# Sliding-window attention and a gated feed-forward block on one core: the order of the prologue's small jobs, of its weight loads, and of batch 1's transposes

## The chip, the cores and the metric

The kernel runs on one core of one Trainium2 chip. The metric is the device time of one execution in microseconds (us). Three runs of the kernel before gave 339.52, 340.06 and 340.07; the median is 340.06.

The core's engines have separate instruction queues and meet through semaphores: PE (TensorE, matmuls and transposes), ACT (ScalarE, exp, Ln, gelu, copies), DVE (VectorE, products and copies), POOL (GpSimd; here above all it issues the loads that convert float32 to bf16) and SP (SyncE; it issues plain DMAs). Each queue is worked off in order, so an instruction that waits also holds up everything queued behind it on its engine.

## The reference

```
scores = q @ k.T / 8 + bias          # per batch and head; S = 576, D = 64, 8 heads, 8 batches
bias   = -slope[h] * (i - j)         # slope[h] = 2 ** -(h + 1)
scores = where(0 <= i - j < 128, scores, -1e9)
x      = softmax(scores) @ v         # put together to x[4608, 512]
out    = (gelu(x @ w_gate) * (x @ w_val)) @ w_out      # d_ff = 1536
```

All inputs and the output are float32; the kernel works in bf16 with float32 accumulation.

## The kernel before, in words

The feed-forward part is the bulk. The 4608 tokens go in nine groups g of 512. For each group and each of 12 tiles f of 128 hidden columns, `gate_val` (line 603) does four matmuls with `w_gate` and four with `w_val`, ACT makes the gelu (line 624), DVE multiplies (line 625) and leaves a hidden tile; `out_part` and `out_half` (lines 647 and 669) then multiply the hidden tiles with `w_out`. Attention for a batch is woven between these matmuls, always for tokens that a later group needs. All PSUM tiles come from one pool of eight banks (`bank`, line 66).

Heads go in pairs c = 0 to 3, with head 2c in partitions 0 to 63 and head 2c + 1 in 64 to 127. Scores need q and k transposed (`qT`, `kT`). The queries of batches 0 and 1 are loaded in "runs" (line 121): each partition holds r consecutive tokens, and after the transposes a copy out of PSUM (`untangle`, line 155, copy in line 158) puts the tokens in order. For batch 1 the first run (n = 0) is tokens 0 to 383 with r = 3, the second (n = 1) tokens 384 to 575 with r = 2.

**Prologue (lines 699 to 831).** Eight DMAs load the first 384 tokens of batch 0's q and k as float32, two heads each (line 713); seven go out on SP, the first of k on ACT. POOL makes `tmpl` (an iota), then copies two elements of the first q load into `mark` (line 720): this holds its queue back until that load has landed. After that POOL issues, in order, the rest of batch 0's q and k, v, and the weights by column ranges (lines 721 to 726): 0 to 128, 128 to 256, 256 to 512, and, further down (lines 833 to 838), 512 to 768, 768 to 1024, 1024 to 1280, then both runs of batch 1's q and k, then 1280 to 1536.

DVE makes small constants: `slope1`, `ones8`, the identity `ident`, `far`, and `dist` (the distances, with a huge number where the mask is, lines 733 to 740). `slopes` (line 748) is one 128x128 diagonal matrix for each head: one DVE product for heads 0 to 3 and one for heads 4 to 7. ACT makes the "decays", exp(-slope x distance) of each head (line 744), from `dist`.

For batch 0 each pair c passes through this: a cast of q and one of k to bf16 (`cast`, line 752, done in line 753), three transposes each (`first`, line 768, PE in line 771) and a copy each (line 158); `biases0` (line 327, PE in line 334) puts slope x distance into two banks with matmuls, `scores0` (line 339, PE in line 212) adds the scores on top, and two exps on ACT follow (line 225, 128x512 each). The code writes out by hand, in lines 792 to 824, which engine does which cast and copy, and in which order. After the four pairs come the sums (`products`), Ln and exp for the reciprocals (lines 571 and 572), the values, the rest of batch 0's scores (eight exps of 128x384), a load of ACT's gelu table, and the gate tiles f = 0 and 1 (for the first 384 tokens), then f = 2 to 8, then the same nine tiles for the other 128 tokens.

**Group 0's end (lines 923 to 953).** Gate tiles 9, 10 and 11 of group 0 are done whole. Behind tiles 9 and 11, `transpose` (line 162) transposes both runs of batch 1's q and k, two pairs at a time: ten transposes and two copies (384 and 192 columns) for each of q and k and each pair, q's copies on ACT, k's on DVE. Then the list in line 893 is worked off in order: scores of batch 1 (`scores`, line 231, s = 0 the first half of the keys, s = 1 the second; each with exps on ACT and a mask product on DVE, line 228), between them halves of the output rows 0 and 1 (`out_half`, six matmuls each, a copy to `osb` in line 679 behind the second half).

Of the kernel before, what the change touches and what calls it, by code (L numbers as in the profile page):

```python
# [8 lines left out]
BF16 = mybir.dt.bfloat16  # L9
AF = mybir.ActivationFunctionType  # L10
ALU = mybir.AluOpType
# [19 lines left out]
def kernel(  # L31
# [34 lines left out]
    def bank():  # L66
        return psum.tile([128, 512], FP32, name="ps")
# [62 lines left out]
    def load_runs(b, n, h0, h1):  # L130
        first, parts, r = RUNS[b][n]
        for what, src in ((0, q), (1, k)):
            nc.gpsimd.dma_start(
                out=runs(what, b, n)[:, h0:h1, :],
                in_=src[b][h0:h1, first:first + parts * r, :].rearrange(
                    "h (p r) d -> p h (r d)", r=r))

    def load_w(lo, hi):
        for dst, src in ((wg, moe_w_gate), (wv, moe_w_val)):
            nc.gpsimd.dma_start(  # L140
                out=dst[:, :, lo:hi],
                in_=src[:, lo:hi].rearrange("(c p) f -> p c f", p=128))

    def transpose_runs(b, n, what, c, ps):
        first, parts, r = RUNS[b][n]
        src = runs(what, b, n)
        p = 64 * what if (b, n) == (0, 1) else 0
        for x in range(r):
            for i in (0, 1):
                nc.tensor.transpose(  # L150
                    out=ps[64 * i:64 * i + 64, parts * x:parts * x + parts],
                    in_=src[:, 2 * c + i, 64 * x:64 * x + 64],
                    identity=ident[p:p + parts, p:p + parts])

    def untangle(copy, b, n, what, c0, c1, ps):
        first, parts, r = RUNS[b][n]
        m = c1 - c0
        copy(out=(qT, kT)[what][b][:, c0:c1, first:first + parts * r].rearrange(
                 "p c (x r) -> p c x r", r=r),
             in_=ps[:, 0:m * parts * r].rearrange("p (c r x) -> p c x r", c=m, r=r))  # L160

    def transpose(b, what, c, copy):
        ps = bank().bitcast(BF16)
        for n, lo in ((0, 0), (1, 384)):
            transpose_runs(b, n, what, c, ps[:, lo:576])
        for n, lo in ((0, 0), (1, 384)):
            untangle(copy, b, n, what, c, c + 1, ps[:, lo:576])

    def transposes_dma(b):
        def of_k():  # L170
# [539 lines left out]
    pairs1 = wo[:, 9:12, :]  # L710
    for h in (0, 2, 4, 6):
        for w, src in ((0, q), (1, k)):
            (nc.scalar if w and h == 0 else nc.sync).dma_start(  # L713
                out=raw[w][h // 4].rearrange("p (h x) -> p h x", h=4)[:, h % 4:h % 4 + 2, :],
                in_=src[0][h:h + 2, 0:384, :].rearrange("h (p r) d -> p h (r d)", r=3))

    nc.gpsimd.iota(tmpl, pattern=[[1, 256]], base=0, channel_multiplier=-1,
                   allow_small_or_imprecise_dtypes=True)
    nc.gpsimd.memset(ones64, 1.0)
    nc.gpsimd.tensor_copy(out=mark, in_=raw[0][0][0:1, 0:2])  # L720
    load_runs(0, 1, 0, 8)
    load_v(0, (0, 1, 2))
    load_w(0, 128)
    load_w(128, 256)
    load_v(0, (3, 4))
    load_w(256, 512)

    for h in range(H):
        nc.vector.memset(slope1[:, h:h + 1], -8.0 * 2.0 ** (-8.0 * (h + 1) / H))
    nc.vector.memset(ones8, 0.0)  # L730
    nc.vector.memset(ones8.rearrange("p (h x) -> p h x", x=40)[:, :, 0:8], 1.0)
    nc.vector.tensor_single_scalar(out=ident, in_=tmpl[:, 0:128], scalar=0.0, op=ALU.is_equal)
    for lo, bound, op in ((0, 0.0, ALU.is_lt), (128, 127.5, ALU.is_gt)):
        nc.vector.tensor_scalar(out=far[:, lo:lo + 128], in0=tmpl[:, lo:lo + 128],
                                scalar1=bound, scalar2=1e9, op0=op, op1=ALU.mult)
# [2 lines left out]
        nc.vector.tensor_tensor(out=dist[half, 0:192], in0=tmpl[half, to], in1=far[half, to], op=ALU.max)  # L738
    for to, n in ((192, 192), (384, 128)):
        nc.vector.tensor_copy(out=dist[:, to:to + n], in_=dist[:, 0:n])  # L740

    def decays(lo, hi):
        for h in range(lo, hi):
            nc.scalar.activation(out=emask[:, h, 0:192], in_=dist[:, 0:192], func=AF.Exp,
                                 scale=-(2.0 ** (-8.0 * (h + 1) / H)))

    def made_slopes(lo, hi):
        nc.vector.tensor_tensor(
            out=slopes[:, lo:hi, :], in0=ident.unsqueeze(1).to_broadcast((128, hi - lo, 128)),
            in1=slope1[:, lo:hi].unsqueeze(2).to_broadcast((128, hi - lo, 128)), op=ALU.mult)  # L750

    def cast(w, c, copy):
        copy(out=pairs0[w][:, :, c, :].rearrange("p x (i d) -> p x i d", i=2),
             in_=raw[w][c // 2].rearrange("p (c i x d) -> p c x i d", c=2, i=2, x=3)[:, c % 2])

    made_slopes(0, 4)

    def masks_of_last_blocks(lo, hi):
        nc.vector.tensor_copy(out=emask[:, lo:hi, 192:384], in_=emask[:, lo:hi, 0:192])
# [8 lines left out]
    def first(w, c, copy, ps):  # L768
        ps = ps.bitcast(BF16)
        for x in range(3):  # L770
            nc.tensor.transpose(out=ps[:, 128 * x:128 * x + 128], in_=pairs0[w][:, x, c, :],
                                identity=ident)
        untangle(copy, 0, 0, w, c, c + 1, ps)
# [19 lines left out]
    held = [bank(), bank()]  # L793
    keep_busy(held[0], 2, 128)
    keep_busy(held[0], 60)
    decays(0, 5)
    cast(0, 0, dve)
    cast(1, 0, act)
    made_slopes(4, 8)
    decays(5, 7)  # L800
    first(0, 0, dve, held[0])
    first(1, 0, act, held[1])
    cast(0, 1, dve)
    cast(1, 1, act)
    decays(7, 8)

    def pair(c, copies, between=None):
        held = [bank(), bank()]
        for w in (0, 1):
            first(w, c, copies[w], held[w])  # L810
            if w == 0 and between:
                between()

    cast(0, 2, dve)
    cast(1, 2, dve)
    scores0((0,), biases0((0,), 4), lambda: pair(1, (dve, act)))
    cast(1, 3, act)
    biases = biases0((1,))
    pair(2, (dve, dve), lambda: cast(0, 3, dve))
    scores0((1,), biases)  # L820
    biases = biases0((2,))
    pair(3, (dve, dve))
    scores0((2,), biases)
    scores0((3,), biases0((3,)))
    row(0)
    sums_a = products(0, sums_first(0))
# [6 lines left out]
    load_w(512, 768)  # L833
    load_w(768, 1024)
    load_w(1024, 1280)
    for n in (0, 1):
        load_runs(1, n, 0, 8)
    load_w(1280, DFF)
    masks, waiting = [], []

    def flush():
# [44 lines left out]
    for t in (qs[0], ks[0]):  # L886
# [3 lines left out]

    acts = (act, act, act, act)
    todo = {
        0: [("table",), ("s", 1, 0, (0, 1)), ("o", 0, 0, 0), ("o", 0, 1, 0), ("s", 1, 0, (2, 3)), ("o", 0, 0, 1), ("s", 1, 1, (0, 1)), ("o", 0, 1, 1), ("s", 1, 1, (2, 3), masks), ("pv+", 1, 0), 4, ("transposes", 2), ("pv+", 1, 1), 4],
        1: [("table",), ("s", 2, 0, (0, 1)), 3, ("s", 2, 0, (2, 3)), 2, ("s", 2, 1, (0, 1)), 2, ("s", 2, 1, (2, 3), masks), ("pv+", 2, 0), 3, ("pv+", 2, 1), 1, 2, ("s2", 3, 0), ("add", 3, 0), 3, ("s2", 3, 2), ("add", 3, 2, None, (0,))],
    }

# [12 lines left out]
    def exp_table():  # L909
        nc.scalar.preload_act_table_set("natural_log_exp_and_others")  # L910

    RUN = {"s": scores, "s2": scores2, "add": add, "sum4": sums4, "gather": gather, "spread": spread_dma, "pv": values, "pv+": values_and_sums,
           "masks": flush, "table": exp_table, "transposes": transposes_dma, "last": out_last, "o": out_half}

    for g in range(NG):
        if 1 <= g < B - 2:
            transposes_dma(3 if g == 1 else g + 2)
        if g == 1:

            nc.gpsimd.tensor_copy(out=mark, in_=kT[1][0:1, 0, 512:514])  # L920
            load_qk(4)
            load_v(3)
        for f in range(9 if g == 0 else 0, NF):
            gate_val(g, f)
            if g == 2 and f == 2:
                add(3, 2, act, (1,))
            if g == 0 and f == 10:
                masks_of_last_blocks(0, 8)
            if g == 0 and f in (9, 11):
                for c in (0, 1) if f == 9 else (2, 3):  # L930
                    for w in (0, 1):
                        transpose(1, w, c, (act, dve)[w])
            if 2 <= g < B - 1:
                if f == (4 if g == 2 else 3):
                    sums4(g + 1)
                if f == (6 if g == 2 else 5):
                    gather(g + 1)
                if f == (8 if g == 2 else 7):
                    spread_dma(g + 1)
                if f == 9 and g + 2 < B:  # L940

                    nc.gpsimd.tensor_copy(out=mark, in_=hid[g][0:1, f, 0:2])  # L942
                    if g + 3 < B:
                        load_qk(g + 3)
                    load_v(g + 2)
        if g == 0:
            nc.gpsimd.memset(Ps[0][:, :, 0:64], 0.0)
            for t in (qs[1], ks[1]):
                nc.gpsimd.memset(t[64:128, 4, :], 0.0)
        for item in steps(g):  # L950
            if isinstance(item, int):
                out_part(g, item)
            else:
                RUN[item[0]](*item[1:])
        store()
        if g == 0:

            nc.gpsimd.tensor_copy(out=mark, in_=qT[0][0:1, 0, 512:514])
            load_qk(3)
            load_v(2)  # L960
# [30 lines left out]
```

## Time and profile before

| what | us |
|---|---|
| median of three runs | 340.06 |
| the profiled execution's own time | 339.51 |
| its span | 337.70 |
| PE busy | 331.6 |
| DVE busy | 192.3 |
| ACT busy | 172.0 |
| POOL busy | 106.6 |
| first Ln of the prologue (line 571) starts | 12.31 |
| gate tile f = 2 starts | 21.02 |
| first scores of batch 1 start | 41.80 |
| group 1 starts | 58.12 |

The span runs from the first to the last instruction of the profiled execution; its own time has 1.81 us more around it. A row of a timeline gives start, duration, engine, line, operation and the tiles that are written and read; "x6" merges six in a row, and a bracket tells how long the engine had been idle and for whom. Instructions on one engine overlap a little: the next can start about 0.1 us before the former's end. The time of a DMA to its landing is counted from the issue on its queue to its completion.

### The profile page before, as it was taken

The numbers are of one execution on the slowest core, as the hardware profiler recorded it, in microseconds if no ns is written. First come the engines' busy times: TensorE is split into PE (matmuls) and PEld (weight loads), VectorE is DVE, ScalarE is ACT, GpSimd is POOL, SyncE is SP. The second block draws the span as 40 slices with busy tenths as digits, with TensorE's granted clock in tenths as the row PEclk, the third lists the DMA queues.
The fourth block names the chain that finished last, engine by engine and source line by source line (L and its number), as shares of the span: only waits on it lengthen the run. The fifth ranks groups of instructions, "written<-read, shape, count | busy, mean of one in ns | idle before, by whom it ended". The sixth has DMA issues, their size and how long they took to land.

```text
span 337.7 us, 8194 instructions
## 1 busy us (share of the span) xinstructions
PE 331.6 (98%) x3342; PEld 169.7 (50%) x3342; DVE 192.3 (57%) x358; ACT 172.0 (51%) x321; POOL 106.6 (32%) x142
## 2 busy tenths in 40 slices
PE   7999999999999999999999999999999999999996
PEld 6677555444554454445544554445444544444443
DVE  7878666335679557945694479536964324303320
ACT  7974597437896339332843375335732233223321
POOL 6975764482292194009500770050000000000000
PEclk9999999999999999999999999999999999999999
DMA  8999999999999799969985999496106110020002
GB/s 209 170 195 192 202 167 188 118 176 153 171 160 149 165 177 204 181 136 145 186 171 102 144 185 183 76 165 93 64 3 142 64 63 1 2 93 31 0 33 93
DMA packets 150026, 43.49 MB, mean 129 GB/s; under 512 B 133572, under 2 KB 142948, under 8 KB 149988
## 3 DMA queue, kind: packets, MB, share of 16 engines
q0 software_dynamic: 107424, 18.10, 70.7%
q1 hardware_dynamic: 39104, 18.55, 24.3%
q10 hardware_dynamic: 3460, 6.32, 8.3%
q8 instruction: 26, 0.43, 0.5%
q14 instruction: 12, 0.10, 0.1%
HBM read 43.65 MB, written 9.53 MB: 157 GB/s over the span
## 4 chain that ended last, share of the span: by engine, by line
PE 91%; ACT 4%; DVE 1%; DMA 1%; issue 1%; SPq 1%; DVEq 0%
PE ps L618 55%; PE ps L654 25%; PE ps L496 4%; PE ps L294 2%; ACT P L225 2%; PE ps L674 2%; PE ps L212 1%; DMA ks<-in_k_dram 1%; PE ps L432 1%; PE ps L688 1%; PE ps L150 1%; ACT rb L572 1%; SPq L713 1%; ACT rb L571 0%; DVE xT L530 0%
## 5 line engine op out<-in xcount | busy, mean ns | idle before, releaser
L625 DVE TENSOR_TENSOR hT<-ps,gelu 128x512 bf16<-128x512 f32 (+3 forms) x119 | 73.9, 637 | 93.0 <-PE ps L618 86.3
L624 ACT ACTIVATE gelu<-ps 128x512 bf16<-128x512 f32 (+3 forms) x119 | 65.5, 558 | 101.4 <-PE ps L618 96.7
L618 PE MATMUL ps<-xT,wg 128*128 128x512 bf16 (+3 forms) x476 | 113.5, 359 | 0.2
L618 PE MATMUL ps<-xT,wv 128*128 128x512 bf16 (+3 forms) x476 | 113.4, 359 | 0.0
L654 PE MATMUL ps<-wo,hT 128*128 128x512 bf16 x396 | 90.3, 380 | 0.0
L618 PEld LDWEIGHTS <-wv 128*128 128x128 bf16 x476 | 45.3, 98 | 48.5
L618 PEld LDWEIGHTS <-wg 128*128 128x128 bf16 x476 | 44.6, 98 | 48.0 <-issue 0.3
L654 PEld LDWEIGHTS <-hT 128*128 128x128 bf16 x396 | 37.1, 98 | 43.6
L225 ACT ACTIVATE P<-ps 128x512 bf16<-128x512 f32 (+1 forms) x108 | 51.2, 579 | 1.3 <-PE ps L212 0.9
L659 ACT COPY osb<-ps 128x512 f32<-128x512 f32 x28 | 16.4, 587 | 50.3 <-PE ps L654 50.3
L228 DVE TENSOR_TENSOR P<-P,emask 128x768 bf16<-128x768 bf16 x60 | 31.3, 556 | 18.6 <-ACT P L225 16.9
L108 POOL DMA_DIRECT2D vb<-in_v_dram x40 | 33.9, 879 | 9.2 <-DMA ks<-in_k_dram 4.3
L108 POOL DMA_DIRECT2D qs<-in_q_dram x30 | 25.5, 865 | 5.8 <-DMA wo<-in_moe_w_out_dram 4.0
L108 POOL DMA_DIRECT2D ks<-in_k_dram x30 | 25.4, 883 | 0.4 <-DMA qs<-in_q_dram 0.3
L942 POOL COPY mark<-hT 1x2 bf16<-1x2 bf16 x4 | 0.7, 176 | 76.7 <-DVE hT L625 76.7
L553 DVE TENSOR_TENSOR xT<-ps,rb 128x512 bf16<-128x512 f32 (+3 forms) x34 | 14.7, 502 | 5.5 <-PE ps L496 5.5
L496 PE MATMUL ps<-P,vb 64*64 64x192 bf16 (+2 forms) x752 | 17.0, 220 | 0.2
L496 PEld LDWEIGHTS <-vb 64*64 64x64 bf16 x752 | 14.4, 107 | 3.1 <-issue 2.6
L380 DVE TENSOR_TENSOR T<-P 64x1024 bf16<-64x1024 bf16 x20 | 13.7, 686 | 0.6
L294 PEld LDWEIGHTS <-kT 64*64 64x64 bf16 x440 | 7.6, 107 | 4.4 <-issue 4.2
L437 DVE RECIPROCAL r<-ps 128x128 f32<-128x128 f32 (+1 forms) x10 | 9.8, 1022 | 0.0
L624 ACT ACT_TABLE_LOAD x7 | 9.0, 1283 | 1.3 <-PE ps L618 1.3
(92 smaller groups left out, 184.2 us busy)
## 6 DMA issues: line engine op xcount, KB each, us to landing
out_dram<-osb SPq DMA_DIRECT2D x35, 256.0 KB
rb<-rd ACTq DMA_DIRECT2D x10, 576.0 KB
vb<-in_v_dram POOLq DMA_DIRECT2D x32, 128.0 KB, 6.7
qs<-in_q_dram POOLq DMA_DIRECT2D x24, 128.0 KB, 5.9
ks<-in_k_dram POOLq DMA_DIRECT2D x24, 128.0 KB, 7.1
wo<-in_moe_w_out_dram POOLq DMA_DIRECT2D x2, 768.0 KB, 14.7
wg<-in_moe_w_gate_dram POOLq DMA_DIRECT2D x5, 256.0 KB, 8.4
wv<-in_moe_w_val_dram POOLq DMA_DIRECT2D x5, 256.0 KB, 9.0
```

The lines of the kernel that those rows point to most:

```text
L108: nc.gpsimd.dma_start(out=t[at:at + n, j, :].rearrange("p (h d) -> p h d", h=H), in_=src[b][:, 128 * j:128 * j + n, :].rearrange("h p d -> ...
L225: nc.scalar.activation(out=dst, in_=src, func=AF.Exp, scale=0.125)
L228: nc.vector.tensor_tensor(out=dst, in0=dst, in1=m, op=ALU.mult)
L294: mm = nc.tensor.matmul(out=ps[64 * x:64 * x + 64, col:col + w], lhsT=keys(b, c, m)[half, :], rhs=qT[b % 2][half, c, q0:q0 + w], start=Tru ...
L380: nc.vector.tensor_tensor(out=to[half, :, x:x + 7:2], in0=P[half, :, 0:10:3], in1=P[half, :, 1:11:3], op=ALU.add)
L496: mm = nc.tensor.matmul(out=out, lhsT=lhsT, rhs=prob(b)[half, c, i, col:col + q1 - q0], start=all(t[2] != u for t in todo[:n]), stop=True, ...
L553: nc.vector.tensor_tensor(out=xT[:, c, at:at + e - a], in0=src, in1=recip[b][:, c, a:e], op=ALU.mult)
L618: nc.tensor.matmul(out=ps, lhsT=w[:, c, 128 * f:128 * (f + 1)], rhs=xT[:, c, t0 + lo:t0 + hi], start=begins, stop=(c == 3), skip_group_che ...
L624: nc.scalar.activation(out=gl[:, 0:n], in_=pg, func=AF.Gelu)
L625: nc.vector.tensor_tensor(out=hid[g][:, f, lo:hi], in0=pv, in1=gl[:, 0:n], op=ALU.mult)
L654: nc.tensor.matmul(out=acc[g], lhsT=hid[g][:, f, 128 * t:128 * (t + 1)], rhs=wo[:, f, :], start=(f == 0), stop=(f == NF - 1))
L659: (nc.vector.tensor_copy if g < B - 2 and t in by_dve.get(g, (0,)) else nc.scalar.copy)(out=osb, in_=acc[g])
```

## The change

- The first load of k goes out on SP like the others, not on ACT.
- `slopes` for heads 4 to 7 is made by POOL, in front of `mark`; that for heads 0 to 3 stays on DVE, behind `dist`; `ones8` is filled behind it.
- All eight decays stand on ACT in front of the first cast.
- DVE makes the last cast of k and ACT the copy of pair 2's keys (before, the other way round, with pair 2's keys on DVE and the last cast of k on ACT); the order of casts, transposes, biases and scores on DVE and PE is new.
- Weight columns 256 to 512 are loaded in two halves for each matrix; batch 1's second run of q and k goes behind the last weights.
- Batch 1's transposes: all of the first run behind tile 9, two pairs to a bank and one copy of 768 columns for two pairs; the second run as an item of the list, behind the scores (1, 0, (2, 3)), four pairs to a bank and one copy of 768 columns each for q (ACT) and k (DVE).

```diff
-    def transpose(b, what, c, copy):
-        ps = bank().bitcast(BF16)
-        for n, lo in ((0, 0), (1, 384)):
-            transpose_runs(b, n, what, c, ps[:, lo:576])
-        for n, lo in ((0, 0), (1, 384)):
-            untangle(copy, b, n, what, c, c + 1, ps[:, lo:576])
+    def transposes(b, n, copies):
+        first, parts, r = RUNS[b][n]
+        m = 1024 // (parts * r) // 2 * 2
+        for c0 in range(0, 4, m):
+            pss = [bank().bitcast(BF16) for _ in range(2)]
+            for what, ps in enumerate(pss):
+                for c in range(c0, c0 + m):
+                    transpose_runs(b, n, what, c, ps[:, parts * r * (c - c0):parts * r * (c - c0 + 1)])
+            for what, ps in enumerate(pss):
+                untangle(copies[what], b, n, what, c0, c0 + m, ps)
...
-            (nc.scalar if w and h == 0 else nc.sync).dma_start(
+            nc.sync.dma_start(
...
+    for h in range(H):
+        nc.vector.memset(slope1[:, h:h + 1], -8.0 * 2.0 ** (-8.0 * (h + 1) / H))
+    nc.vector.tensor_single_scalar(out=ident, in_=tmpl[:, 0:128], scalar=0.0, op=ALU.is_equal)
+
+    def made_slopes(lo, hi, by):
+        by.tensor_tensor(
+            out=slopes[:, lo:hi, :], in0=ident.unsqueeze(1).to_broadcast((128, hi - lo, 128)),
+            in1=slope1[:, lo:hi].unsqueeze(2).to_broadcast((128, hi - lo, 128)), op=ALU.mult)
+
+    made_slopes(4, 8, nc.gpsimd)
     nc.gpsimd.tensor_copy(out=mark, in_=raw[0][0][0:1, 0:2])
...
-    load_w(256, 512)
+    load_w(256, 384)
+    load_w(384, 512)
...
+    made_slopes(0, 4, nc.vector)
+    nc.vector.memset(ones8, 0.0)
+    nc.vector.memset(ones8.rearrange("p (h x) -> p h x", x=40)[:, :, 0:8], 1.0)
...
-    decays(0, 5)
+    decays(0, 8)
     cast(0, 0, dve)
     cast(1, 0, act)
-    made_slopes(4, 8)
-    decays(5, 7)
     first(0, 0, dve, held[0])
+    biases = biases0((0,))
     first(1, 0, act, held[1])
     cast(0, 1, dve)
     cast(1, 1, act)
-    decays(7, 8)
-
-    def pair(c, copies, between=None):
-        held = [bank(), bank()]
-        for w in (0, 1):
-            first(w, c, copies[w], held[w])
-            if w == 0 and between:
-                between()
-
+
+    def pair_1():
+        held = [bank(), bank()]
+        first(0, 1, dve, held[0])
+        first(1, 1, act, held[1])
+
+    scores0((0,), biases, pair_1)
+    biases = biases0((1,))
+    held = [bank(), bank()]
     cast(0, 2, dve)
     cast(1, 2, dve)
-    scores0((0,), biases0((0,), 4), lambda: pair(1, (dve, act)))
-    cast(1, 3, act)
-    biases = biases0((1,))
-    pair(2, (dve, dve), lambda: cast(0, 3, dve))
-    scores0((1,), biases)
-    biases = biases0((2,))
-    pair(3, (dve, dve))
-    scores0((2,), biases)
+    cast(0, 3, dve)
+    first(0, 2, dve, held[0])
+    cast(1, 3, dve)
+    scores0((1,), biases, lambda: first(1, 2, act, held[1]))
+    held3 = [bank(), bank()]
+    first(0, 3, dve, held3[0])
+    scores0((2,), biases0((2,)))
+    first(1, 3, dve, held3[1])
     scores0((3,), biases0((3,)))
...
-    for n in (0, 1):
-        load_runs(1, n, 0, 8)
+    load_runs(1, 0, 0, 8)
     load_w(1280, DFF)
+    load_runs(1, 1, 0, 8)
...
-        0: [("table",), ("s", 1, 0, (0, 1)), ("o", 0, 0, 0), ("o", 0, 1, 0), ("s", 1, 0, (2, 3)), ("o", 0, 0, 1), ("s", 1, 1, (0, 1)), ("o", 0, 1, 1), ("s", 1, 1, (2, 3), masks), ("pv+", 1, 0), 4, ("transposes", 2), ("pv+", 1, 1), 4],
+        0: [("table",), ("s", 1, 0, (0, 1)), ("o", 0, 0, 0), ("o", 0, 1, 0), ("s", 1, 0, (2, 3)), ("T", 1, 1, (act, dve)), ("o", 0, 0, 1), ("s", 1, 1, (0, 1)), ("o", 0, 1, 1), ("s", 1, 1, (2, 3), masks), ("pv+", 1, 0), 4, ("transposes", 2), ("pv+", 1, 1), 4],
...
-            if g == 0 and f in (9, 11):
-                for c in (0, 1) if f == 9 else (2, 3):
-                    for w in (0, 1):
-                        transpose(1, w, c, (act, dve)[w])
+            if g == 0 and f == 9:
+                transposes(1, 0, (act, dve))
```

More of the change, by code (lines that the diff above doesn't have):

```diff
@@ L725 @@
     load_v(0, (3, 4))
-    load_w(256, 512)
[L728 to L732, printed above, removed]
+    load_w(256, 384)
+    load_w(384, 512)
     for lo, bound, op in ((0, 0.0, ALU.is_lt), (128, 127.5, ALU.is_gt)):
@@ L745, in decays @@
                                  scale=-(2.0 ** (-8.0 * (h + 1) / H)))
[L747 to L750, printed above, removed]
     def cast(w, c, copy):
@@ L754, in cast @@
              in_=raw[w][c // 2].rearrange("p (c i x d) -> p c x i d", c=2, i=2, x=3)[:, c % 2])
-    made_slopes(0, 4)
     def masks_of_last_blocks(lo, hi):
@@ L912 @@
     RUN = {"s": scores, "s2": scores2, "add": add, "sum4": sums4, "gather": gather, "spread": spread_dma, "pv": values, "pv+": values_and_sums,
-           "masks": flush, "table": exp_table, "transposes": transposes_dma, "last": out_last, "o": out_half}
+           "masks": flush, "table": exp_table, "transposes": transposes_dma, "T": transposes, "last": out_last, "o": out_half}
     for g in range(NG):
```

## The prediction

> **What bounds the kernel now.** I read the page first, then the chain of waits in order of time, then the timelines of PE, ACT, DVE and POOL up to 62 us, then each DMA's time to landing.
>
> ```profile
> span 337.7 us, 8194 instructions
> PE 331.6 (98%) x3342; PEld 169.7 (50%) x3342; DVE 192.3 (57%) x358; ACT 172.0 (51%) x321; POOL 106.6 (32%) x142
> PEclk9999999999999999999999999999999999999999
> ```
>
> PE is busy for 98% at full clock. By the view of waits PE itself waits 2.0 us in the whole run, all before 20 us. From 21.02 us, where the third gate tile (f = 2) begins, the chain is PE work nearly end to end. So the change can only win what brings f = 2 forward, and loses whatever it opens behind it. What sets 21.02 is ACT:
>
> ```profile
> 4.24 0.51 ACT L753 CAST ks<-wo 128x384 bf16<-128x384 f32 x1 [0.28 <-DMA wo<-in_k_dram]
> ...
> 8.71 0.51 ACT L753 CAST ks<-ks 128x384 bf16<-128x384 f32 x1 [1.01 <-DMA ks<-in_k_dram]
> 9.12 3.30 ACT L225 ACTIVATE P<-ps 128x512 bf16<-128x512 f32 x6
> 12.31 0.88 ACT L571 ACTIVATE rb<-ps 128x384 f32<-128x384 f32 x2
> ...
> 15.79 3.14 ACT L225 ACTIVATE P<-ps 128x384 bf16<-128x384 f32 x8
> 18.95 1.28 ACT L624 ACT_TABLE_LOAD   x1
> ```
>
> Start, duration, engine, line, tiles. From 8.71 to the gelus behind the table load ACT never rests: f = 2 starts 8.71 us after the first Ln (12.31), whatever that is. The question of the prologue is when that Ln starts: behind the last of eight exps of 0.53 each. The last two need pair 3's scores, and these its keys' copy:
>
> ```profile
> 7.66 1.00 DVE L158 COPY qT<-ps 128x384 bf16<-128x384 bf16 x2
> 8.58 0.79 DVE L753 CAST qs<-qs 128x384 bf16<-128x384 f32 x1
> 9.29 0.54 DVE L158 COPY kT<-ps 128x384 bf16<-128x384 bf16 x1
> 9.80 0.56 DVE L158 COPY qT<-ps 128x384 bf16<-128x384 bf16 x1
> 10.28 0.55 DVE L158 COPY kT<-ps 128x384 bf16<-128x384 bf16 x1
> ```
>
> DVE is full from 7.03 to 10.83, then S3 (pair 3's scores; S0 to S3 below) runs at 10.88. Thus ACT and DVE are level; moving a job between them pays only if the other has room.
>
> **The change, part by part.** Times are of the profiled execution.
>
> *Decays first.* One decay (128x192 exp) costs 0.258: five, each 0.348 long, take 1.38 from 2.59. They need dist, written at 2.51, so losing ACT's own DMA issue (0.75 to 1.26) brings the table load to about 0.8 but the decays only to 2.55. Eight of them end at 4.70, so the first key cast starts at about 4.62, not 4.24: +0.38. Then as before: T(1,0), copy of kT at 5.57 (was 5.19), S0 at 6.10 (was 5.72). Decays 5 to 7 that leave later gaps give nothing back before S0.
>
> *Casts and copies.* T(0,1) is queued behind S0 on PE, so DVE copies qT of pair 1 at about 6.88 (6.10, 0.34 until the transposes start, 0.34 of them, 0.1 from their end to a copy, as at 4.77 and 4.88 for pair 0). Behind it stand four casts and three copies in one row: q2, k2, q3, copy q2, k3, copy q3, copy k3. Copies are spaced 0.48. DVE casts lasted 0.42, 0.63, 0.42, 0.71, 0.79; spaced 0.08 less I take 0.56 (bounds 0.34 and 0.71). End of the last: 6.88 + 4 x 0.48 + 4 x 0.56 + 0.07 = 11.11, against 10.83 before. With the quickest casts ACT and PE set it: T(0,2) 7.84, S1 8.02, exp 8.54, copy of kT pair 2 on ACT 9.02, S2 9.55, T(1,3) 9.9, copy ends 10.85. So S3 starts at 11.16 (10.90 to 11.5), the two exps at 11.68 and 12.20, the Ln at 12.73: **+0.42** on 12.31 (+0.14 to +0.75). ACT's wait of 1.01 at 8.71 is gone, but comes back as waits for S1 and S3. The keys land in time: key cast 3 is due at 9.5, and pair 3's keys landed at 8.69.
>
> *Slopes on GpSimd.* DVE loses 0.67 at 4.29, where nothing waits. POOL's product has no row. From below its memset of 128x512 (0.53), from above three such passes (two reads, a write, 1.6): from 1.5 it ends by 2.0 to 3.1, before POOL's mark waits out q's first landing (3.98). First use is at 8.6. Cost zero, if it leaves DVE alone; see rival 2. *The first key load on SP*: all later issues come 0.5 later, yet landings 0.57 apart (6.43 to 7.00) at 0.5 per issue show a backlog; zero. q alone in front may land, and start POOL's loads, up to 0.5 earlier (half of the two first loads' time).
>
> *Weights 256 to 512 in halves.* Each DMA costs POOL about 0.75. The four 128 KB loads landed 0.7 to 0.8 apart with constant latency, so POOL's issue paces them; 256 KB loads land 1.3 apart with growing latency:
>
> ```profile
> wg<-in_moe_w_gate_dram POOLq DMA_DIRECT2D x1, 128.0 KB, 6.3
> wg<-in_moe_w_gate_dram POOLq DMA_DIRECT2D x1, 256.0 KB, 6.1
> wv<-in_moe_w_val_dram POOLq DMA_DIRECT2D x1, 256.0 KB, 10.1
> ```
>
> Four halves at 0.75 instead of two wholes at 1.3: everything behind lands 0.4 later, or 0.1 earlier if POOL starts 0.5 earlier. Before, wv for f = 8 landed at 28.75 (18.67 + 10.1) and was needed at 29.46, the least slack of f = 2 to 8: 0.7. With f = 2 at +0.42, still 0.7: zero. But it caps any gain at 0.3 to 0.8.
>
> The Trainium skill ("DMA: Bandwidth & Descriptors", Specifications) asks for 512 B per piece at least, with read-modify-write below. A half row is 256 B in the written type, which speaks against the halves; estimated at double the time, 2.6 us would be added and f = 8 would wait about 1.5. This case's 0.75 against 0.65 per 128 KB does not show it.
>
> *Second run of q, k behind the weights.* wg and wv from 1280 landed at 36.5 and 37.8 for a need at 37.10 and 37.97, slack 0.2; now two loads of 1.1 to 1.25 less stand before them. A cover, not a gain, while f = 2 does not come earlier.
>
> *Batch 1's transposes.* Two blocks of 40 (1.14 each) become 48 at f = 9 and 32 behind the scores of (1, 0, (2, 3)). By columns the 32 are 0.73, by count 0.9; the total is unchanged. But the copies change place:
>
> ```profile
> 46.53 0.56 DVE L228 TENSOR_TENSOR P<-P,emask 128x768 bf16<-128x768 bf16 x1 [0.54 <-ACT P L225]
> 47.30 0.56 DVE L228 TENSOR_TENSOR P<-P,emask 128x768 bf16<-128x768 bf16 x1 [0.21 <-ACT P L225]
> 47.77 0.68 DVE L679 COPY osb<-ps 128x512 f32<-128x512 f32 x1
> ```
>
> On PE the same stretch reads:
>
> ```profile
> 45.23 0.53 PE L212 MATMUL ps<-qT,kT 64*64 64x192 bf16 x16
> 45.68 1.47 PE L674 MATMUL ps<-wo,hT 128*128 128x512 bf16 x6
> 47.08 0.53 PE L212 MATMUL ps<-qT,kT 64*64 64x192 bf16 x20
> ```
>
> The key copy now stands on DVE behind both masks of that block: it starts 2.54 after its scores (47.77 - 45.23). Its 768 columns: copies of 384 and 192 columns took 0.548 and 0.348, so 0.148 + 768 x 1.04 ns = 0.95. The next scores can start 3.55 after. PE has only 0.45 + 0.8 + 1.40 = 2.65 of work until then. **PE waits 0.9** (0.8 to 1.0, as the 32 take 0.9 or 0.73). Against before: the distance between the two score blocks grows by 1.70 (3.55 against 47.08 - 45.23), and the first comes 0.89 earlier (2.29 of transposes in front of it become 1.40). Net **+0.8**. The query copy on ACT (about 0.8, behind exps ending 47.27) ends sooner. Behind the stall PE is full to the end, so nothing returns it. wo's halves landed at 41.6 and 45.4; 0.4 later they are due just when needed.
>
> **Sum**: +0.42 + 0.8 = +1.2. The profiled execution took 339.51 (span 337.70 and 1.81 around it), so 340.7; the median of the runs shown, 340.06, is 0.55 above that one, and on it the change gives **341.3**.
>
> **Rivals.**
> 1. *The prologue is even*: the decays in front hide behind idle time of ACT, and quick casts win DVE's 0.3 back; T's wait stays. For it: DVE casts of 0.42. Against: S0's path. +0.5 to +0.8, 340.6 to 340.9.
> 2. *GpSimd holds up dist.* Its product starts about 1.5, just when DVE makes far and dist (1.40 to 2.51). Casts from 0.42 to 0.79 while POOL issued DMAs show DVE can lose 0.37 an instruction; a whole product of 0.68 to 1.6 is the outer bound. Decays, S0 and all behind come 0.7 to 1.3 later: +1.9 to +2.5, about 342.3.
>  The Trainium skill ("SBUF — State Buffer", SBUF: two separate sides) says that a GpSimd operation and a DVE one with two SBUF inputs exclude each other for the whole instruction; that is this rival's worst case, and no run here shows such a pair.
> 3. *ACT's lost 1.01 is won, weights cap it*: f = 2 comes 0.5 to 0.8 earlier, T's wait gives that back: -0.0 to +0.3, 340.1 to 340.4.
> 4. *Faster.* ACT's waits (1.01 at 8.71, 0.28 at 4.24) and its DMA issue (0.51) all vanish: 1.8 at most off the Ln, less T's 0.8: -0.4 to -1.0, about 339.2. It decides if pair 3's key copy ends before 9.5 and the weights keep up. Against: DVE's row of seven jobs, and wv of f = 8.
>
> **How the numbers follow.** Forecast 0.42, rival 1 0.18, rival 2 0.20, rival 3 0.13, rival 4 0.07. 0.2% of 340.06 (what a measurement can tell from no change) is 0.68. Faster: rival 4, 0.07. Same: rival 3 and half of rival 1, 0.22. Slower: the rest, 0.71. The range from 339.9 to 342.5 leaves out rival 4 and the upper half of rival 2.
>
> **What would show it.** S0 at 6.1 and the first Ln at 12.7, f = 2 at 21.4; DVE without a gap from 6.9 to 11.1; the halves 0.75 apart; behind the 32 transposes a PE wait of 0.8 to 0.9 on DVE's copy of kT of 0.95. It is wrong if that copy ends before the six out matmuls, if ACT has copied and exponentiated earlier than 12.3, or if DVE's first two-input operations grow longer.

## The result, and the profile after

The changed kernel took **352.73 us** (median of 6; 351.06 to 354.52), the kernel before in the same comparison 340.06 (median of 6; 339.52 to 341.27): a ratio of 1.0368, interval 1.0343 to 1.0394. It is slower, as forecast, but by 12.7 us and not by 1.2. The profiled execution is the longest of the six, 354.52 with a span of 352.7, 15.0 more than before's.

One thing belongs to the reading of these times: the changed kernel zeroes a part of batch 1's q and k (heads 4 to 7 of tokens 512 to 575) before it transposes them, so those scores are computed from zeros; E2 and E3 below share that. How it comes about is the main finding.

The head of the page:

```profile
span 352.7 us, 8140 instructions
PE 331.2 (94%) x3296; PEld 170.6 (48%) x3338; DVE 191.2 (54%) x352; ACT 171.6 (49%) x316; POOL 108.7 (31%) x145
PEclk9999995999999999999999999999999999999999
```

PE's busy time is the same (331.2 against 331.6), so no work was added: PE stood still (and part of the 331.2 is the same work at a lower clock, as shown below). One digit of the clock row has fallen to 5, at 53 to 62 us, inside the stretch where batch 1's attention starts. PE's waits name the culprit; each row gives who waits, for whom, the total, how often and the longest:

```profile
PE ps L150 <- POOL qs L952: 8.7, 1, 8.7
PE ps L678 <- DMA wo<-in_moe_w_out_dram: 1.3, 1, 1.3
```

A transpose (line 150) waited 8.7 us for a write of `qs` by POOL (line 952). That row has no counterpart in before. On PE's timeline it stands here:

```profile
45.00 2.76 PE L678 MATMUL ps<-wo,hT 128*128 128x512 bf16 x12 [1.27 <-DMA wo<-in_moe_w_out_dram]
47.69 0.53 PE L216 MATMUL ps<-qT,kT 64*64 64x192 bf16 x16
48.14 0.36 PE L150 MATMUL ps<-ident,qs 96*64 96x96 bf16 x8
57.18 0.53 PE L150 MATMUL ps<-ident,qs 96*64 96x96 bf16 x8 [8.67 <-POOL qs L952]
...
60.95 0.85 PE L216 MATMUL ps<-qT,kT 64*64 64x192 bf16 x20
```

Of q's sixteen transposes the first eight (pairs 0 and 1) run at 48.14; the other eight (pairs 2 and 3, so heads 4 to 7) start at 57.18. From one score block to the next it is 13.26 us, where before it was 1.85. POOL's timeline shows what it did meanwhile:

```profile
48.98 0.87 POOL L108 DMA_DIRECT2D qs<-in_q_dram  x1 [2.88 <-DMA wo<-in_moe_w_out_dram]
50.23 1.56 POOL L108 DMA_DIRECT2D qs<-in_q_dram  x2 [0.38 <-issue]
51.77 4.21 POOL L108 DMA_DIRECT2D ks<-in_k_dram  x5
56.02 0.53 POOL L950 MEMSET P<- 128x512 bf16 x1
56.60 0.52 POOL L952 MEMSET qs<- 64x512 bf16 x1
```

Lines 949 to 952 stand in the program just in front of group 0's list and clear `qs[1]` and `ks[1]` for a later batch, in partitions 64 to 127 and the last 512 columns. Batch 1's second run lies in partitions 0 to 95 and the last 1024 columns of the same tiles. Where they overlap are heads 4 to 7 of the run's last 64 tokens. Before, all transposes of batch 1 were in front of the memset; now the second run's are behind it in the program, so they wait for it, and the memset is last in POOL's row, behind the ten loads of batch 2's q and k, which are themselves held back until `w_out` has landed.

The clock in this stretch, per window: span, then busy time of PE, PEld, DVE, ACT and POOL, the granted clock, the DMA share and GB/s.

```profile
48.60:57.20 8.60, 0.02 (x2) 0.03 (x2) 1.12 (x2) 1.13 (x3) 7.75 (x11) 0.76 2.39 153
58.30:61.00 2.70, 2.48 (x11) 0.76 (x14) 0.96 (x1) 0.30 (x1) 0.00 (x0) 0.50 0.24 15
61.00:64.00 3.00, 3.00 (x33) 1.42 (x36) 1.81 (x3) 1.64 (x5) 0.00 (x0) 0.62 0.25 87
```

While PE idled the clock fell to half (mean 0.76 over the idle 8.6), and PE then worked at half clock until about 63 (0.62 over 3 us).

In the prologue the first Ln starts at 14.54 (before 12.31) and f = 2 at 23.24 (before 21.02). ACT and DVE:

```profile
3.22 2.13 ACT L757 ACTIVATE emask<-wo 128x192 bf16<-128x192 bf16 x8 [1.20 <-DVE wo L748]
...
13.57 1.08 ACT L229 ACTIVATE P<-ps 128x512 bf16<-128x512 f32 x2 [1.51 <-PE ps L216]
```

```profile
1.75 1.44 DVE L748 TENSOR_TENSOR wo<-tmpl,far 64x192 bf16<-64x192 f32 x2
...
11.63 0.43 DVE L761 CAST ks<-ks 128x384 bf16<-128x384 f32 x1 [1.52 <-DMA ks<-in_k_dram]
```

The two products that make `dist` took 1.44 together instead of 0.72, so the decays start at 3.22 instead of 2.59; and DVE waits 1.52 for pair 3's keys to land, at 11.63, where before they were there at 8.71. By stretches the 15.0 are, to 0.1: +2.2 until f = 2, -0.8 until batch 1's first scores (16 of each 40 transposes are gone from there; -0.9 was forecast), +1.1 from there to the first output matmuls (the wait for `w_out`), +11.4 from the scores (2, 3) to the next scores, +1.1 of half clock until group 1 starts (73.07 against 58.12). Behind that nothing differs.

### The profile page after: what moved, and what is told of

The parts are those of the page before. It is cut to its first block, busy times and chain, and to the rows that moved or that the text cites. A ratio compares the mean times of both kernels' runs of the same rounds, so it can differ in the third digit from the quotient of the medians.

```text
span 352.7 us, 8140 instructions
## 1 busy us (share of the span) xinstructions
PE 331.2 (94%) x3296; PEld 170.6 (48%) x3338; DVE 191.2 (54%) x352; ACT 171.6 (49%) x316; POOL 108.7 (31%) x145
## 4 chain that ended last, share of the span: by engine, by line
PE 82%; DMA 7%; ACT 4%; issue 2%; POOL 2%; DVE 1%; SPq 1%; DVEq 0%
PE ps L622 49%; PE ps L658 23%; DMA wo<-in_moe_w_out_dram 5%; PE ps L500 3%; PE ps L298 2%; DMA ks<-in_k_dram 2%; ACT P L229 2%; PE ps L678 1%; POOL ks L108 1%; PE ps L216 1%; SPq L717 1%; PE ps L436 1%; PE ps L692 1%; POOL qs L108 1%; ACT rb L576 1%
## 5 line engine op out<-in xcount | busy, mean ns | idle before, releaser
L622 PE MATMUL ps<-xT,wg 128*128 128x512 bf16 (+3 forms) x461 | 111.9, 359 | 0.8
L658 PE MATMUL ps<-wo,hT 128*128 128x512 bf16 x375 | 87.8, 380 | 2.0 <-issue 1.3
L622 PEld LDWEIGHTS <-wv 128*128 128x128 bf16 x476 | 45.3, 98 | 48.5
L150 PE MATMUL ps<-ident,qs 128*64 128x128 bf16 (+1 forms) x40 | 1.9, 232 | 8.7 <-POOL qs L952 8.7
```

Source lines behind the costliest of these rows:

```text
L622: nc.tensor.matmul(out=ps, lhsT=w[:, c, 128 * f:128 * (f + 1)], rhs=xT[:, c, t0 + lo:t0 + hi], start=begins, stop=(c == 3), skip_group_che ...
L658: nc.tensor.matmul(out=acc[g], lhsT=hid[g][:, f, 128 * t:128 * (t + 1)], rhs=wo[:, f, :], start=(f == 0), stop=(f == NF - 1))
```

## The experiments

Each expectation names its theories and rivals by letters. The main ones are these. P: the memset on POOL explains most of the loss. C: the half clock behind the wait has a price of its own. For the prologue, L: the late `dist` sets the first Ln; R: the late keys set it; D, D1 and D2: what the prologue's new order costs by itself. E1 to E4 were timed beside the kernel before at 339.75 us, E5 to E8 beside 339.90, E9 to E12 beside 339.69.

**E1, the memsets behind the list.**

```diff
         if g == 0:
             nc.gpsimd.memset(Ps[0][:, :, 0:64], 0.0)
-            for t in (qs[1], ks[1]):
-                nc.gpsimd.memset(t[64:128, 4, :], 0.0)
         for item in steps(g):
...
         if g == 0:
+            for t in (qs[1], ks[1]):
+                nc.gpsimd.memset(t[64:128, 4, :], 0.0)
```

> The changed kernel with one thing moved: the two memsets of lines 951 and 952 (partitions 64 to 127 of the last 512 columns of batch 1's q and k buffers) stand behind the list of group 0, not in front of it. In the changed kernel they zero heads 4 to 7 of tokens 512 to 575 of batch 1 before the moved transposes read them; here those are the loaded values. Theory P (the moved transposes wait for the POOL memset, which is queued behind ten loads, 8.67 us, and PE then runs about 2.3 us at half clock): the wait and the slow stretch go, the score blocks behind the second-run transposes start 3.5 after the ones in front (13.3 in the changed kernel), time about 342. Rival W (w_out's second half, landed at 48.7, or DVE's queue would hold the same instructions nearly as long anyway): 348 or more.

342.95 us (341.33 to 343.54), 1.0084 [1.0065, 1.0103]: 9.8 less than the changed kernel. Theory P holds. PE's timeline now shows the wait that the prediction was about:

```profile
46.82 1.47 PE L678 MATMUL ps<-wo,hT 128*128 128x512 bf16 x5
48.35 0.28 PE L216 MATMUL ps<-qT,kT 64*64 64x192 bf16 x4
49.12 0.45 PE L216 MATMUL ps<-qT,kT 64*64 64x192 bf16 x16 [0.49 <-DVE kT L158]
```

The scores before stand at 45.56; sixteen of the next twenty start at 49.12, 3.56 later, behind DVE's copy of 0.95. The first four need only the first run's keys and go ahead.

**E2, the changed kernel with 150 matmuls of 128 columns, whose result nothing uses, put in front of the second run's transposes**, so that PE is not idle while it waits.

```diff
-            pss = [bank().bitcast(BF16) for _ in range(2)]
+            pss = [bank() for _ in range(2)]
+            keep_busy(pss[0], 150 * n, 128)
+            pss = [ps.bitcast(BF16) for ps in pss]
```

> The changed kernel with 150 dummy matmuls of 128 columns on PE in front of the second-run transposes (about 8.6 us that fall into the wait of 8.67); as in the changed kernel the memsets zero heads 4 to 7 of tokens 512 to 575 of batch 1's q and k first. Theory C (after an idle stretch PE is granted half its clock, and that costs o(0,0,1), the scores and o(0,1,1) 1.27 + 0.32 + 0.75 = 2.3 us): with PE busy through the wait the clock stays at 1.00 and the time is about 350.4. Rival (these matmuls are slow for another reason, such as loads or banks that come late): unchanged, about 352.7.

350.34 us (349.68 to 351.6), 1.0288 [1.0221, 1.0355]: 2.4 less than the changed kernel at a granted clock of 1.000 (0.985 there). What follows the wait is back at its usual durations:

```profile
55.80 1.47 PE L680 MATMUL ps<-wo,hT 128*128 128x512 bf16 x5
57.20 0.53 PE L218 MATMUL ps<-qT,kT 64*64 64x192 bf16 x20
```

From the first output matmul behind the wait to group 1 it is 12.44 us here (55.80 to 68.24), and 14.79 in the changed kernel (58.28 to 73.07). So about 2.4 us are the price of half clock, though by the times alone the two intervals overlap a little (E2's ends at 1.0355, the changed kernel's begins at 1.0343).

**E3, the kernel before with batch 1's transposes alone changed** (the new `transposes`, its calls, the list's new item; nothing of the prologue, the loads or the memsets).

```diff
-            if g == 0 and f in (9, 11):
-                for c in (0, 1) if f == 9 else (2, 3):
-                    for w in (0, 1):
-                        transpose(1, w, c, (act, dve)[w])
+            if g == 0 and f == 9:
+                transposes(1, 0, (act, dve))
...
-        0: [("table",), ..., ("s", 1, 0, (2, 3)), ("o", 0, 0, 1), ...],
+        0: [("table",), ..., ("s", 1, 0, (2, 3)), ("T", 1, 1, (act, dve)), ("o", 0, 0, 1), ...],
```

> The kernel before with only the transposes changed (first run behind tile 9, second run as an item of the list); as in the changed kernel the memsets zero heads 4 to 7 of tokens 512 to 575 of batch 1's q and k before they are transposed. Theory P: the end of the wait is set by POOL's queue (memsets at 53.2 in the kernel before, 56.6 in the changed one), so nearly all of the loss is here: about 351, 3.4 less on the end of the wait but with an earlier start. Rival S (the parts add up, the prologue's 2.2 and the late w_out's 1.1 are separate): 12.7 less 3.3 on 340.1, 349.4 or less.

350.57 us (350.13 to 351.97), 1.0297 [1.023, 1.0364]. This one part brings 10.1 of the 12.5 us (by ratios), with the same row on PE:

```profile
54.67 0.53 PE L150 MATMUL ps<-ident,qs 96*64 96x96 bf16 x8 [8.55 <-POOL qs L951]
```

**E4, E3 with the memsets behind the list.** On E3's edit comes E1's:

```diff
-            for t in (qs[1], ks[1]):
-                nc.gpsimd.memset(t[64:128, 4, :], 0.0)
         for item in steps(g):
...
+            for t in (qs[1], ks[1]):
+                nc.gpsimd.memset(t[64:128, 4, :], 0.0)
```

> The kernel before with the transposes changed as in the changed kernel and the two memsets behind the list of group 0. The prediction's step (key copy on DVE behind two masks, 0.95 long, PE waits 0.8): 340.9. Rival (PE does not feel it, the transposes cost the same in the new place): 340.1. Third: POOL's later memsets delay the loads of batch 3, above 341.5.

340.75 us (339.54 to 341.52), 1.0023 [1.0006, 1.004]: 0.8 by the ratio, with 0.2 to 1.4 in its interval, beside the 0.8 of the prediction's own step. The scores are again 3.56 apart (45.18 and 48.74). But the way there differs in one thing: with fewer transposes in front, the first output matmuls are reached at 41.5 and wait 0.99 for `w_out`, so the 0.83 that the first scores gain (40.97 against 41.80) is lost again there:

```profile
42.49 2.76 PE L678 MATMUL ps<-wo,hT 128*128 128x512 bf16 x12 [0.99 <-DMA wo<-in_moe_w_out_dram]
```

In this profile group 1 starts at 59.70, 1.58 later than before.

**E5, E1 with the first key load back on ACT.**

```diff
-            nc.sync.dma_start(
+            (nc.scalar if w and h == 0 else nc.sync).dma_start(
```

> e1 (the changed kernel with the memsets behind) with the first key load issued on ACT again. In e1 pair 3's keys landed at 10.75 (8.7 in the kernel before) and the first Ln started at 13.65 (12.31). Theory R (the eight loads on one queue, and POOL's loads starting earlier, make the last keys land late, and they set the Ln): keys land at about 9, then DVE's row of seven jobs behind the copy of pair 1's queries sets the Ln at about 13.2: 0.45 less than e1, 342.5. Rival L (only the late dist counts): as e1, 342.95.

341.2 us (340.98 to 341.86), 1.0045 [1.003, 1.006]: 1.75 less than E1 by the medians, 1.3 by the ratios. POOL's `mark` is at 4.12 (E1 3.28), so its loads start 0.8 later, and the last key cast no longer waits, though `dist` is as late as in E1. DVE's row in E1, then in E5:

```profile
10.75 0.43 DVE L761 CAST ks<-ks 128x384 bf16<-128x384 f32 x1 [0.18 <-DMA ks<-in_k_dram]
```

```profile
9.81 0.41 DVE L761 CAST ks<-ks 128x384 bf16<-128x384 f32 x1
```

The Ln starts at 13.25, as theory R has it (13.2; E1 13.65). The time fell by more than its 0.45, and by the profiles the rest isn't the prologue's: f = 2 starts 0.4 earlier than in E1 (21.95 against 22.36) and group 1 0.5 (59.57 against 60.08). Another 1.6 of E1's profiled execution arise between 108.8 and 136.3 us, where E1 takes 27.5 us, with PE waits at line 298, and E5 takes 25.9 for the same work. What causes that is open.

**E6, E1 with the slopes of heads 4 to 7 back on DVE**, behind those of heads 0 to 3.

```diff
-    made_slopes(4, 8, nc.gpsimd)
...
     made_slopes(0, 4, nc.vector)
+    made_slopes(4, 8, nc.vector)
```

> e1 with the slopes of heads 4 to 7 made on DVE behind those of heads 0 to 3 and not on POOL. Theory L (the POOL product keeps DVE's two-input operations from running: line 748 took 1.44 instead of 0.72 and ACT's decays began at 3.23 instead of 2.59): 0.72 and 2.55 are back; if dist alone set the Ln, 0.7 less than e1, 342.25. Rival R (the last keys' landing at 10.75 sets the Ln): decays early, but the Ln as in e1, 342.95.

342.48 us (342.16 to 342.94), 1.0083 [1.0066, 1.01]: 0.5 less than E1, not told apart from it. `dist`'s products took 0.72 again and the decays started at 2.5, but the last key cast ran at 10.66 and the Ln at 13.56 (E1 13.65). The late `dist` is real, and hidden by the later keys: against L and for this run's rival R.

**E7, E5 and E6 together.**

```diff
-            nc.sync.dma_start(
+            (nc.scalar if w and h == 0 else nc.sync).dma_start(
...
-    made_slopes(4, 8, nc.gpsimd)
...
+    made_slopes(4, 8, nc.vector)
```

> e5 and e6 together. What is left of the prologue is the order: eight decays in front, the casts and copies dealt out anew, halves of the weights. Theory D (the prediction's sum for this part): first Ln at 12.73, f = 2 at 21.4, 0.4 above the transposes alone (e4, 340.75): 341.2. Rival (the order costs nothing once the lock and the late keys are gone): 340.75 or less.

341.39 us (340.82 to 342.17), 1.0049 [1.0031, 1.0066], level with E5. The Ln starts at 13.39; 12.73 was expected. PE's timeline shows the start of the delay, here and in E6, which has the same order:

```profile
5.36 0.63 PE L338 MATMUL ps<-wo 128*128 128x512 bf16 x1 [0.22 <-issue]
5.78 0.53 PE L777 MATMUL ps<-ident,ks 128*128 128x128 bf16 x3
```

```profile
5.18 0.38 PE L338 MATMUL ps<-wo 128*128 128x512 bf16 x1
5.39 0.33 PE L777 MATMUL ps<-ident,ks 128*128 128x128 bf16 x3
```

The first biases (line 338), matmuls of 512 columns, now stand in front of the first keys' transposes (line 777), which start at 5.39 in E6 where 5.19 was expected (before 4.81). Neither theory had that. In E7 they start at 5.78, since PE itself was slower in this execution: its biases took 0.63 and its transposes 0.53, in E6 0.38 and 0.33. S0 follows at 6.29 in E6 and at 6.88 in E7 (6.1 was forecast). So of E7's lateness about 0.2 goes with the biases and 0.6 with a PE that was slow at the start. E2's prologue has the same slow PE for longer (biases of 1.06 at 8.18), and its Ln starts at 14.25 with a last key cast at 10.44 that waits for nothing.

**E8, E1 with `mark` reading the first key load instead of the first query load**, so that POOL starts later, with all first loads still on SP.

```diff
-    nc.gpsimd.tensor_copy(out=mark, in_=raw[0][0][0:1, 0:2])
+    nc.gpsimd.tensor_copy(out=mark, in_=raw[1][0][0:1, 0:2])
```

> e1 with POOL's mark reading the first key load instead of the first query load, so that POOL's loads start some 0.6 later while all eight loads stay on SP. It tells the two halves of theory R apart. If POOL's early start (3.4 against 4.0) makes the last keys late: they land at about 9.5 and the time falls to about 342.5, as e5. If it is the single queue: keys at 10.7 as in e1, and 342.95 or more.

342.29 us (341.05 to 343.42), 1.0073 [1.0045, 1.0101]. In the profile `mark` is at 3.93, the last key cast at 9.82, the Ln at 13.13 and f = 2 at 21.83, as good as E5's; the time lies between E1's and E5's and its interval holds E1's ratio. So the early start of POOL's loads is a likely part of why the keys are late. It is not settled as the whole: in E6 these loads start at 4.00, almost as late as here (4.12), and the last key cast still waits until 10.66.

**E9, the kernel before with the casts, copies, biases and scores dealt out as in the changed kernel**, with loads, slopes and decays left as they were and the first biases behind both first transposes.

```diff
     first(1, 0, act, held[1])
+    biases = biases0((0,))
...
+    cast(0, 3, dve)
+    first(0, 2, dve, held[0])
+    cast(1, 3, dve)
+    scores0((1,), biases, lambda: first(1, 2, act, held[1]))
```

> The kernel before with only the casts and copies of the prologue dealt out as in the changed kernel: the decays stay split (5, 2, 1), the slopes and all loads as before, and the first biases stay behind the transposes of the first keys. Theory D1 (in the prologue's new order it is the decays and the first biases in front that cost, the dealing itself is level): S0 at 5.72, the first Ln at 12.1 to 12.4, no difference from the kernel before. Theory D2 (DVE's row of four casts and three copies behind pair 1's query copy costs by itself): first Ln 0.4 or more later, +0.4.

339.69 us (339.37 to 341.04), 0.9993 [0.9974, 1.0013]. The Ln starts at 12.5 (before 12.31), f = 2 at 21.18. The new dealing is level.

**E10, the kernel before with weight columns 256 to 512 in halves, nothing else.**

```diff
-    load_w(256, 512)
+    load_w(256, 384)
+    load_w(384, 512)
```

> The kernel before with only the weight columns 256 to 512 in two halves. The prediction's step (POOL's issue paces 128 KB loads at 0.75, all that is behind lands 0.4 later; least slack 0.7 up to f = 8, 0.2 at f = 10): +0.2 at most. Rival (pieces of 256 B cost double): 2.6 later, f = 8 waits and the time rises by 1.5 or more.

340.31 us, 1.001 [0.9988, 1.0032]. No difference that can be measured. In the profile PE waits 0.5 and 0.3 in front of the two matrices of f = 10, the tile for which the expectation had the least slack (0.2); the wait of 1.5 that doubled transfers would have brought isn't there.

**E11, E4 with the second run's transposes three items earlier in the list**, behind the scores (1, 0, (0, 1)).

```diff
-        0: [..., ("s", 1, 0, (0, 1)), ("o", 0, 0, 0), ("o", 0, 1, 0), ("s", 1, 0, (2, 3)), ("T", 1, 1, (act, dve)), ...],
+        0: [..., ("s", 1, 0, (0, 1)), ("T", 1, 1, (act, dve)), ("o", 0, 0, 0), ("o", 0, 1, 0), ("s", 1, 0, (2, 3)), ...],
```

> e4 with the second-run transposes two items earlier in the list, behind the scores (1, 0, (0, 1)), so that DVE's key copy stands behind the first two masks and has the twelve out matmuls (2.7 us) as cover. Theory (the copy behind the masks is what holds PE 0.8 in e4): PE's wait in front of the scores of s = 1 is gone and the time is that of the kernel before. Rival (the wait of 0.99 for w_out's first half that e4 shows, or the later memsets, cost as well): as e4, +1.0.

339.61 us, 0.9995 [0.9974, 1.0017]. The wait for DVE's key copy is gone, the one for `w_out` is down to 0.2, and the kernel is level with before.

**E12, the parts that cost nothing, together**: E9's dealing, E11's transposes, and the second run behind the last weights. On E9's and E11's edits comes:

```diff
-    for n in (0, 1):
-        load_runs(1, n, 0, 8)
+    load_runs(1, 0, 0, 8)
     load_w(1280, DFF)
+    load_runs(1, 1, 0, 8)
```

> What the runs so far leave standing: e9's dealing of casts and copies, e11's place for the second-run transposes with the memsets behind the list, and batch 1's second run behind the last weights; decays, slopes, first key load and weights 256 to 512 as in the kernel before. If the weights of tiles 10 and 11 and w_out's first half were close to holding PE, and the dealing of e9 brings the first Ln forward, it beats the kernel before by up to 0.3; otherwise it equals it.

339.73 us, 1.0000 [0.9978, 1.0022]. Level with before; no version here beats it. The profiled execution, 1.4 slower than the median, has new small PE waits: 1.1 without a releaser at line 500, 0.3 for `v` and 0.4 for `w_out`.

## Why the prediction was wrong, point by point

By ratios, on 340.06: the memset's wait with its half clock is 9.7 (changed kernel less E1: 0.0284), the transposes' own wait 0.8 (E4: 0.0023), the prologue with its loads 2.1 (E1 less E4: 0.0061). The three fill the 12.5 that the ratio gives by construction. The traces bear out the first: 13.26 us between the score blocks in the changed kernel, 3.56 in E1. They do not bear out the 2.1 as the size of the prologue: f = 2 starts 1.35 later in E1 than in E4 (22.36 against 21.01), but group 1 only 0.4 (60.08 against 59.70), as E4 waits for `w_out`, and the 1.6 of E1's profile behind 108 us lie in a part that the change leaves alone. The +1.1 for `w_out` in the profiled changed kernel is in none of the three; E1, with the same loads, has no such wait.

**The step that failed is "Batch 1's transposes".** It took the new place of the second run's transposes through the queues of PE, ACT and DVE and through `w_out`'s landing, and made of it +0.8. It did not ask what they were moved past on POOL: the memsets of the tile that they read. The profile of before had the price all the time, in POOL's timeline:

```profile
48.43 4.19 POOL L108 DMA_DIRECT2D ks<-in_k_dram  x5
...
53.25 0.52 POOL L949 MEMSET qs<- 64x512 bf16 x1
```

There the memset ended at 53.77, with nobody waiting. Transposes due at about 46 and made to depend on it wait for some 7.8 us; 8.67 and 8.55 were measured. The distance that the step did count was right: 3.55 from scores to scores forecast, 3.56 in E1 and E4. That its net +0.8 was measured too (E4) is partly luck. Its gain of 0.89 in front was lost to a wait for `w_out`, which the step had down as due just when needed, so that group 1 starts 1.58 later in E4's profile. And PE's wait for the key copy is 0.49, not 0.8 to 1.0, as four score matmuls go ahead. "Behind the stall PE is full to the end" also holds, but it is full at half clock for the first 6 us: 2.4 that no step had.

**The first key load on SP, "zero", failed too, by a size that stays open.** A backlog of landings was taken as proof that issue times don't matter. From 4 to 7 us the core's DMAs moved 316 GB/s in before, 327 in E5 and 332 in E7 (two queues), 255 in the changed kernel and 249 in E1 (one queue, POOL earlier). The prediction expected that POOL's loads might start up to 0.5 earlier, and did not ask what they would hold up; they started 0.7 earlier (3.52 against 4.22). Pair 3's last key cast, waiting for its landing, ran at 11.63 in the changed kernel and at 10.75 in E1 instead of 8.71. Keeping the load on ACT brings f = 2 forward by 0.4 (E5 against E1); how much the single queue and how much POOL's start had to do with it, E6 and E8 leave open.

**Decays first, +0.42 for the prologue's order.** In the changed kernel S0 came at 6.72, not 6.1, as `dist` was late: the first key cast ran at 5.26 instead of 4.62, and the transposes right behind it. The first biases in front of the keys' transposes were overlooked; they show where `dist` is in time, with S0 at 6.29 in E6. From S0 to the Ln E7 takes 6.51, and 6.63 was forecast, so the row of casts and copies was sized about right, and E9 shows that dealing it out anew costs nothing by itself. (One bound was added up wrong: with casts of 0.71 that row ends at 11.71, which puts S3 at 11.76 and not at 11.5 at most.) By the times E7 is 0.6 to 0.9 above E4, with intervals that overlap. The decays in front, the place of the biases and the halves are not separated further by any run.

**Slopes on GpSimd, "cost zero, if it leaves DVE alone".** It did not: rival 2's mechanism took place, with 0.72 on `dist` (forecast 0.7 to 1.3). Its consequence was smaller than that rival's +1.9, as the keys were later still; E6 against E1 shows 0.5 at most. The product itself, 1.08 us, lay within the bounds of 0.53 and 1.6. The Trainium skill ("SBUF — State Buffer", SBUF: two separate sides) has such a pair exclude each other for the whole instruction. The run agrees: the first of the two DVE products took 1.07 instead of 0.36 and ended 0.2 behind POOL's product.

**Halves** and **second run behind the weights**, both at zero, were right as far as the runs can tell (E10; no wait in E12 for the run's landing). **Rival 1** (even prologue) describes E9, not the changed kernel. **Rivals 3 and 4** needed an earlier f = 2 and did not occur.

## What to carry to other kernels

When an instruction moves in the program, list every writer and reader of its tiles that it moves past, on every engine, and read in the profile of before when each of them *ends*: an instruction that nobody waits for today may be late by many microseconds and cost nothing. A padding memset belongs as far behind, or as far in front, as its tile allows, and not at the end of a row of load issues. A wait of PE costs more than its length once it is long enough for the clock to drop.

## What the runs showed of the hardware that was not expected

- **The clock after a wait.** PE idled from 48.5 to 57.2 us. The granted clock was 1.00 until 53 us, 0.53 from 53 to 54 and 0.50 from 54 to 57: about 4 us at half (a mean of 0.76 over 8.6 is 0.24 x 8.6 / 0.5 = 4.1). PE then worked at half until about 63 (0.38 x 3 / 0.5 = 2.3 behind 61). Kept busy in E2, it stayed at 1.000 and the kernel was 2.4 us shorter. The Trainium skill ("TensorE: Matmul & The Clock Gate", Part 1: The HAM clock gate) gives at least one window of about 3.4 us for either change. The fall, some 4.6 us into the wait, fits that; the way back took some 6 us here, of which PE was not busy throughout (2.48 of 2.70 us from 58.3 to 61).
- **PE at the start.** The same three transposes took 0.53 us in E7 and 0.33 in E6, at nearly the same time (5.78 and 5.39). How long PE's first matmuls are slow differed from one profiled execution to the next, in E2 up to about 10 us, and the prologue with it.
- **GpSimd and DVE.** A GpSimd product of two inputs (128x512, 1.08 us) beside two DVE products of 64x192 lengthened these from 0.72 to 1.44 together, all of it on the first of the two; without it (E6, E7) they took 0.72.
- **Eight loads on one queue, or seven and one.** From 4 to 7 us the DMAs moved 302 to 332 GB/s with a key load on ACT (before, E3 to E5, E7, E9 to E12) and 249 to 282 without (the changed kernel, E1, E2, E6, E8). In the latter POOL's loads also start 0.1 to 0.8 us earlier than before, and E8, at 282, has its last keys as early as E5.
